# Window-attention backward: turning the gradients of the first quads on TensorE behind the last pair of the step before, instead of inside the softmax

## The chip, the cores and the metric

The kernel runs on one core of a Trainium2 chip. The metric is the device time of one execution in microseconds. Before the change the median of four runs is 1995.97 us (1989.96, 1994.89, 1997.04 and 1997.92). Engines are named as in the profile: PE is TensorE, DVE VectorE, ACT ScalarE, POOL GpSimd, SP SyncE (here a queue that only issues DMAs). PEld is PE's loading of weights, which runs beside the matmuls.

## The reference

The input is an image of 256 x 256 positions with 384 channels, cut into 1024 windows of 8 x 8 = 64 positions. Each window is one attention with a single head. Wanted are the output and the gradients with respect to `x`, `wqkv` and `wo`, all in bfloat16.

```
xw  = windows of x                        # (1024, 64, 384)
q, k, v = split(xw @ wqkv)
p   = softmax(q k^T * 384**-0.5)
out = (p v) @ wo
out_1, out_2, out_3 = gradients of out by x, wqkv, wo, for the given grad_out
```

## The kernel before

The weights are multiplied with each other once, at the start (`A = wq wk^T * scale`, `AT` its transpose, `B = wv wo`, `BT` its transpose), so that a window needs only the tokens `x` and the incoming gradient `d`. Eight windows form a quad: four tiles `t` of 128 tokens, each with two windows. There are 128 quads, `sts[0]` to `sts[127]`. Per quad, `xq` and `dq` are the tokens and the gradients as loaded; `xT` and `dT` are the same turned, with the channels on the partitions.

`step(c, b, a, ahead)` (line 330) works on three quads at once. The main loop calls it for i = -1 to 128 with c = quad i-1, b = quad i, a = quad i+1 and ahead = quad i+3. All engines run in the order in which the code is written (`manual_schedule`, line 417). In one step:

- For b: `scores` (line 179) multiplies `yz` with `xT` into the PSUM tile `sd`; `soft` 0 to 5 (line 191) are the softmax and its backward part on DVE and ACT, ending in the tile `ps`; between them `uv` (line 230) makes two products per tile, `uq` and `vq`, each brought out of PSUM by ACT (line 238). `turn` (line 240) turns `ps` into `PS` by a DMA.
- For a: `project(0)` (line 160), called z here, multiplies `BT` with all of `dT`, ACT brings it out (line 170). `project(1)`, called y, multiplies `A` with `xT` (brought out at line 172). Both go to the tile `yz`, which `scores` of the next step needs whole, and which `to_tokens` turns by a DMA into `tok`.
- For c: `attend` (line 250) makes the outputs `o` and `d` and the operands of the weight gradients, for tiles (0, 1) between z and y and for tiles (2, 3) at the end of the step. ACT brings out `o` and `d` (line 273), POOL issues their stores.
- From step 4 on, `filler` (line 322) runs the products of the weight gradients (`gf_group`, groups of three quads) twice in each step, on PE and DVE. Steps 0 to 3 have none.

The turned gradients `dT` come from a DMA on SP (`load_turn`, line 129) for quads 4 to 127. For quads 0 to 3 (`G_ON_PE` = 4) PE makes them: `turn_on_pe` (line 137) issues, for each tile, three PE transposes into a PSUM tile `pt` (line 141) and one copy out (lines 91 and 89: DVE for t = 0 and 2, ACT for t = 1 and 3). Quad 0 is turned before the loop. Quads 1 to 3 are turned by `A(grad_turn)` in steps 0 to 2, between the products of tile 2 and tile 3 in `uv`. `woT_sb`, the turned `wo` that only the end of the kernel uses, is made in step 0 behind z: nine transposes (line 97), two copies on DVE and one on ACT.

All PSUM tiles come from `ring`, eight slots of one bank. A slot is given out in the order in which the code frees the slots; a product into a slot waits until the copy out of the slot's last content has ended. `dT` has two slots, `xT` three, `xq` ten.

Of the kernel before, what the change touches and what calls it, by code (L numbers as in the profile page):

```python
# [22 lines left out]
def kernel(  # L23
# [38 lines left out]
    wo_sb = grp.tile([P, CK, C], BF16, tag="Wq", name="wo_sb")  # L62
    wT = [grp.tile([P, CK, C], BF16, tag="Uq", name="wT") for part in range(3)]
    woT_sb = const.tile([P, CK, C], BF16)
# [9 lines left out]
    def fetch_weights():  # L74
        nc.sync.dma_start(out=w_sb[:, :, columns(2)], in_=w_in[:, :, columns(2)])
        nc.scalar.dma_start(out=wo_sb[:], in_=wo.rearrange("(m p) n -> p m n", p=P))
        for k in (0, 1):
            nc.scalar.dma_start(out=w_sb[:, :, columns(k)], in_=w_in[:, :, columns(k)])

    def warm_up(n):  # L80
        zero = B_sb[:].rearrange("p m c -> p (m c)")[:, 0:4 * P]
        nc.vector.memset(zero, 0.0)
        for i in range(n):
            pt = ring.tile([P, 4 * P], F32, tag="r", name="warm")
            nc.tensor.matmul(pt[:], lhsT=zero[:, 0:P], rhs=zero, start=True, stop=True)

    def copy_out(i, out, in_):
        if i % 2:
            nc.scalar.copy(out=out, in_=in_)
        else:  # L90
            nc.vector.tensor_copy(out=out, in_=in_)  # L91

    def turn_blocks(dst, src, first=0):
        for k in range(CK):
            pt = ring.tile([P, C], BF16, tag="r", name="pt")
            for m in range(CK):
                nc.tensor.transpose(pt[:, m * P:(m + 1) * P], src[:, m, (first + k) * P:(first + k + 1) * P], ident[:])
            copy_out(k, dst[:, k, :], pt[:])

    def weight_product(dst, left, right, sc):  # L100
        for mr in range(CK):
            pc = ring.tile([P, C], F32, tag="r", name="pc")
            for mc in range(CK):
                nc.tensor.matmul(pc[:], lhsT=left[:, mc, mr * P:(mr + 1) * P], rhs=right[:, mc, :],
                                 start=(mc == 0), stop=(mc == CK - 1))
            if sc is not None:
                nc.scalar.activation(out=dst[:, mr, :], in_=pc[:], func=ACT.Copy, scale=sc)
            else:
                copy_out(mr, dst[:, mr, :], pc[:])

    def weight_rest():
        weight_product(B_sb, wT[2], wo_sb, None)
        weight_product(AT_sb, wT[1], wT[0], scale)
# [8 lines left out]
    def load(st):  # L122
        st["xq"] = xq = grp.tile([P, QUAD, C], BF16, tag="xq", name="xq", bufs=2 * GQ + 4)
        st["dq"] = dq = qp.tile([P, QUAD, C], BF16, tag="dq", name="dq", bufs=6)
        for t in range(QUAD):
            nc.sync.dma_start(out=xq[:, t, :], in_=windows(x, st, 2 * t))
            nc.gpsimd.dma_start(out=dq[:, t, :], in_=windows(grad_out, st, 2 * t))  # L127

    def load_turn(st):
        st["xT"] = qp.tile([P, QUAD, CK, P], BF16, tag="xT", name="xT", bufs=3)  # L130
        st["dT"] = qp.tile([P, QUAD, CK, P], BF16, tag="dT", name="dT")
        for src, dst, on_pe in (("dq", "dT", G_ON_PE), ("xq", "xT", X_ON_PE)):
            if st["i"] >= on_pe:
                nc.sync.dma_start_transpose(out=st[dst][:].rearrange("p t m k -> p (t m) k"),
                                            in_=st[src][:].rearrange("p t c -> p (t c)"))

    def turn_on_pe(st, src, dst):
        for t in range(QUAD):
            pt = ring.tile([P, CK, P], BF16, tag="r", name="pt")
            for m in range(CK):  # L140
                nc.tensor.transpose(pt[:, m, :], st[src][:, t, m * P:(m + 1) * P], ident[:])
            copy_out(t, st[dst][:, t, :, :], pt[:])

    def grad_turn(st):
        if 0 < st["i"] < G_ON_PE:
            turn_on_pe(st, "dq", "dT")

    ALL = False
    split = [ALL]
# [38 lines left out]
    def over_k(ap, n=P):  # L188
        return ap.unsqueeze(2).broadcast_to([n, QUAD, WT])

    def soft(st, step):
        sd = st["sd"]
        if step == 0:
# [113 lines left out]
    def gf_group(sts, last=False):  # L307
        n = len(sts) * QUAD
        for f in range(2):
            if last:  # L310
                final[f] = grp.tile([P, CK, C], BF16, tag="Uq", name="GFb")
            for ma in range(CK):
                pw = ring.tile([P, C], F32, tag="r", name="pg")
                for i in range(n):
                    st, t = sts[i // QUAD], i % QUAD
                    product(pw[:], st["xq"][:, t, ma * P:(ma + 1) * P], st["UW"[f] + "q"][:, t, :], i == 0, i == n - 1)
                nc.vector.tensor_tensor(out=GF_acc[:, f, ma, :], in0=pw[:], in1=GF_acc[:, f, ma, :], op=ALU.add)  # L317
                if last:
                    nc.vector.tensor_copy(out=final[f][:, ma, :], in_=GF_acc[:, f, ma, :])
                yield  # L320

    def filler(n):
        while n and fill:
            try:
                next(fill[0])
                n -= 1
            except StopIteration:
                fill.pop(0)

    def step(c, b, a, ahead):  # L330


        def on(st):
            return (lambda f, *r: f(st, *r)) if st is not None else (lambda f, *r: None)
        C_, B, A = on(c), on(b), on(a)
        B(scores)
        B(soft, 0)
        if b is not None and c is None:
            weight_rest()
        B(uv, 0, 0)  # L340
        B(uv, 0, 1)
        B(soft, 1)
        B(uv, 1, 0)
        B(uv, 1, 1)
        B(soft, 2)
        B(soft, 3)
        B(uv, 2, 0)
        B(uv, 2, 1)
        A(grad_turn)
        B(uv, 3, 0)  # L350
        B(uv, 3, 1)
        B(soft, 4)
        for mo in range(CK):
            A(project, 0, mo)
        if b is not None and c is None:
            turn_blocks(woT_sb, wo_sb)
        B(soft, 5)
        B(turn)
        if ahead is not None:
            load(ahead)  # L360
        filler(1)
        C_(attend, (0, 1))
        split[0] = True
        for mo in range(CK):
            A(project, 1, mo)
        A(to_tokens)
        filler(1)
        split[0] = ALL
        C_(attend, (2, 3))

    G_ON_PE, X_ON_PE = 4, 1
    EV = {"z": "AAA", "y": "AAA", "u": "AAAA", "v": "AAAA", "o": "AAAA", "U": "DDDD", "W": "DDDD", "d": "AAAA"}
    quads = [(row, col) for row in range(0, H, 2 * WIN * QUAD) for col in range(0, W, WIN)]
    sts = [{"at": q, "i": i} for i, q in enumerate(quads)]
# [42 lines left out]
    with tc.manual_schedule(engines=MANUAL):  # L417
        fetch_weights()
        warm_up(9)
        load(sts[0])  # L420
        make_identity(nc, ident[:])
        load(sts[1])
        load(sts[2])
        load_turn(sts[0])
        load_turn(sts[1])
        turn_blocks(wT[2], w_sb, 2 * CK)
        weight_product(BT_sb, wo_sb, wT[2], None)
        turn_on_pe(sts[0], "dq", "dT")
        turn_on_pe(sts[0], "xq", "xT")
        turn_blocks(wT[0], w_sb, 0)  # L430
        turn_blocks(wT[1], w_sb, CK)
        weight_product(A_sb, wT[0], wT[1], scale)
        nc.vector.memset(GF_acc[:], 0.0)
        held = []
        last = None
        get = lambda i: sts[i] if 0 <= i < n else None
        for i in range(-1, n + 1):
            if 0 <= i < n - 2:
                load_turn(sts[i + 2])
            step(get(i - 1), get(i), get(i + 1), get(i + AHEAD) if i >= 0 else None)  # L440
            if i > 0:
                held.append(sts[i - 1])
                sts[i - 1] = None
            if held and i == n:
                last = gf_group(held, True)
            elif len(held) == GQ:
                fill.append(gf_group(held))
                held = []
        split[0] = False
        filler(1 << 30)  # L450
        weight_gradients(last)
# [30 lines left out]
```

## Time and profile before

| | |
|---|---|
| median of four runs | 1995.97 us |
| the profiled execution | 1997.92 us, of which the span of the trace is 1996.1 us |
| PE busy | 1970.3 us, 99% of the span |
| ACT busy | 1462.8 us, 73% |
| DVE busy | 1260.3 us, 63% |
| granted TensorE clock | 0.998 in the mean |

The start of the matmuls of `scores` (tile `sd`) marks the steps: 18.32 us for step 0, then 33.99, 48.97, 63.25, 76.14, 91.26 and 106.39 for steps 1 to 6. From step 4 on a step takes 15.13 us in most cases. The profile lists busy time of each engine, a timeline of its instructions (start, duration, engine, line, operation; in square brackets the idle time before it and what ended it), and the waits summed by engine and releaser. A row with "x3" holds three instructions that follow each other, and its duration is that of all three.

### The profile page before, as it was taken

The page shows a single profiled execution, that of the slowest core. Times are in us where ns is not written, and L with a number is a line of the kernel's source. Part 1 is how long each engine was busy: PE and PEld are TensorE (multiplying, and loading weights), DVE is VectorE, ACT ScalarE, POOL GpSimd, SP SyncE. Part 2 cuts the span into 40 slices and gives each one's busy share as a digit, 9 for nine tenths or more (in the row PEclk, how much of TensorE's full clock was granted, in tenths as well). Part 3 has the DMA queues.
Part 4 walks back from the last instruction along what each step waited for, and adds up shares of the span by engine and source line. Part 5 has one row for each costly group of instructions (what it writes and reads, how often), then busy time and mean ns, then how long its engine had stood idle before and what let it go on. Part 6 is the DMA issues. An engine that isn't in the chain of part 4 may idle for free.

```text
span 1996.1 us, 52529 instructions
## 1 busy us (share of the span) xinstructions
PE 1970.3 (99%) x19487; PEld 1126.2 (56%) x19487; DVE 1260.3 (63%) x2860; ACT 1462.8 (73%) x3357; POOL 1124.6 (56%) x2054
## 2 busy tenths in 40 slices
PE   8999999999999999999999999999999999999999
PEld 4555555555555555555555555555555555555555
DVE  4666665666656666666665666666666665666666
ACT  6877776777777777777776777777777776777774
POOL 3655555555555555555655565556555655555553
PEclk9999999999999999999999999999999999999999
DMA  7999999999999999999999999999999999999994
GB/s 170 217 202 223 211 221 207 214 208 223 216 219 220 221 207 224 219 216 215 219 220 211 216 208 225 216 220 220 223 211 222 215 220 201 213 230 217 214 210 107
DMA packets 1036032, 423.66 MB, mean 212 GB/s; under 512 B 918016, under 2 KB 1011200, under 8 KB 1035776
## 3 DMA queue, kind: packets, MB, share of 16 engines
q1 hardware_dynamic: 935984, 267.85, 81.2%
q0 software_dynamic: 98304, 151.39, 30.9%
q8 instruction: 152, 2.49, 0.6%
q10 hardware_dynamic: 1488, 1.08, 0.2%
q14 instruction: 104, 0.85, 0.2%
HBM read 101.84 MB, written 101.84 MB: 102 GB/s over the span
## 4 chain that ended last, share of the span: by engine, by line
PE 89%; DMA 8%; issue 2%; POOL 1%; ACT 0%; DVE 0%; SPq 0%; ACTq 0%; POOLq 0%
PE pj L156 33%; PE pg L156 12%; PE pj L154 12%; PE pg L154 11%; PE pd L267 6%; PE pu L262 5%; DMA dT<-dq 5%; PE sd L156 4%; PE pw L262 4%; DMA PS<-ps 1%; DMA out_dram<-o 1%; POOL dq L127 0%; DMA dq<-in_grad_out_dram 0%; PE pd L262 0%; PE pe L384 0%
## 5 line engine op out<-in xcount | busy, mean ns | idle before, releaser
L301 POOL DMA_DIRECT2D out_dram<-o x256 | 139.5, 545 | 668.3 <-ACT o L273 665.4
L317 DVE TENSOR_TENSOR GF_acc<-pg,GF_acc 128x384 f32<-128x384 f32 x258 | 144.0, 558 | 527.9 <-PE pg L154 373.9
L273 ACT CAST o<-po 128x384 bf16<-128x384 f32 x512 | 221.7, 486 | 248.0 <-issue 245.7
L156 PEld LDWEIGHTS <-xT 128*128 128x128 bf16 x3072 | 291.7, 98 | 183.2 <-issue 1.5
L156 PE MATMUL pj<-AT_sb,xT 128*128 128x384 bf16 x1536 | 333.3, 326 | 0.8 <-DVE dT L91 0.8
L156 PE MATMUL pj<-B_sb,xT 128*128 128x384 bf16 x1536 | 333.4, 326 | 0.0
L127 POOL DMA_DIRECT2D dq<-in_grad_out_dram x512 | 273.0, 539 | 83.9 <-DMA out_dram<-o 35.3
L156 PE MATMUL pj<-dT,BT_sb 128*128 128x512 bf16 x1152 | 270.9, 380 | 12.7 <-DMA dT<-dq 7.6
L154 PE MATMUL pj<-xT,A_sb 128*64 128x512 bf16 x2304 | 271.9, 381 | 0.0
L238 ACT CAST uq<-pj 128x384 bf16<-128x384 f32 x512 | 247.6, 484 | 30.0 <-PE pj L156 25.9
L238 ACT CAST vq<-pj 128x384 bf16<-128x384 f32 x512 | 249.9, 488 | 2.2
L273 ACT CAST d<-pd 128x384 bf16<-128x384 f32 x512 | 226.9, 509 | 0.2 <-ACT o L273 0.2
L156 PEld LDWEIGHTS <-xq 128*128 128x128 bf16 x1572 | 153.9, 98 | 115.3 <-issue 1.4
L154 PEld LDWEIGHTS <-xq 128*64 128x64 bf16 x3000 | 167.8, 110 | 89.1 <-issue 0.2
L216 ACT COPY ps<-Pb 64x256 bf16<-64x256 bf16 x256 | 103.3, 403 | 149.7 <-DVE Pb L213 148.2
L172 ACT CAST yz<-pj 128x512 bf16<-128x512 f32 x384 | 208.0, 653 | 2.0 <-PE pj L154 1.6
L170 ACT CAST yz<-pj 128x512 bf16<-128x512 f32 x384 | 206.7, 638 | 3.0 <-PE pj L156 1.5
L156 PEld LDWEIGHTS <-BT_sb 128*128 128x128 bf16 x1152 | 111.5, 98 | 140.0 <-DMA dT<-dq 14.2
L154 PEld LDWEIGHTS <-A_sb 128*64 128x64 bf16 x2304 | 132.1, 110 | 98.2 <-issue 2.2
L156 PE MATMUL pg<-Uq,xq 128*128 128x384 bf16 x1032 | 182.1, 327 | 0.0
L262 PE MATMUL pu<-xq,PS 64*64 64x384 bf16 x1024 | 174.9, 335 | 3.8 <-DMA PS<-ps 3.5
L267 PE MATMUL pd<-tok,ps 128*64 128x384 bf16 x1024 | 177.7, 344 | 0.0
(87 smaller groups left out, 3391.0 us busy)
## 6 DMA issues: line engine op xcount, KB each, us to landing
xq<-in_x_dram SPq DMA_DIRECT2D x512, 96.0 KB, 4.1
dq<-in_grad_out_dram POOLq DMA_DIRECT2D x512, 96.0 KB, 4.0
out_dram<-o POOLq DMA_DIRECT2D x256, 96.0 KB, 4.3
out_dram<-o POOLq DMA_DIRECT2D x512, 48.0 KB, 4.4
out_dram<-d POOLq DMA_DIRECT2D x256, 96.0 KB, 4.5
out_dram<-d POOLq DMA_DIRECT2D x512, 48.0 KB, 4.5
tok<-yz SPq DMA_TRANSPOSE x128, 8.3
PS<-ps SPq DMA_TRANSPOSE x128, 4.8
```

Source lines behind the costliest of these rows:

```text
L127: nc.gpsimd.dma_start(out=dq[:, t, :], in_=windows(grad_out, st, 2 * t))
L154: nc.tensor.matmul(out[h], lhsT=lhsT[:, h], rhs=rhs, start=start, stop=stop)
L156: nc.tensor.matmul(out, lhsT=lhsT, rhs=rhs, start=start, stop=stop)
L170: ENG[EV["z"][mo]](out=yz[:, mo, :, 0:4:3, :], in_=pj[:])
L172: ENG[EV["y"][mo]](out=yz[:, mo, :, 1:3, :], in_=pj[:])
L216: nc.scalar.copy(out=ps[h, :, w, :], in_=Pb[h, :, :])
L238: cp(out=dst[:, t, :], in_=pj[:])
L262: nc.tensor.matmul(at[o, :], lhsT=turned(st, lhs, t, h), rhs=st[rhs][h, t, :], **{"start": True, "stop": True, **fl})
L267: nc.tensor.matmul(pd[outer if w == 0 else 1 - outer][o, :], lhsT=st["ps"][:, t, w, :], rhs=st["tok"][:, :, t, w, :], **flags)
L273: nc.scalar.copy(out=sb[:], in_=src[outer][:])
L301: nc.gpsimd.dma_start(out=windows(dst, st, 2 * t0 + 1), in_=sb[:])
L317: nc.vector.tensor_tensor(out=GF_acc[:, f, ma, :], in0=pw[:], in1=GF_acc[:, f, ma, :], op=ALU.add)
```

## The change

`grad_turn` goes away. The main loop calls `turn_on_pe` itself, right after `step`, for quad i+2 where that is quad 1, 2 or 3. Quad 1 is therefore turned at the end of step -1, quad 2 at the end of step 0 and quad 3 at the end of step 1, each behind the last thing that the step does on PE and ahead of the next step's `scores`. `turn_blocks(woT_sb, wo_sb)` moves from step 0 to the end of step 1, behind the turn of quad 3. The number of instructions on each engine is the same; SP's and POOL's queues hold the same instructions in the same order.

```diff
-    def grad_turn(st):
-        if 0 < st["i"] < G_ON_PE:
-            turn_on_pe(st, "dq", "dT")
...
         B(uv, 2, 0)
         B(uv, 2, 1)
-        A(grad_turn)
         B(uv, 3, 0)
         B(uv, 3, 1)
         B(soft, 4)
         for mo in range(CK):
             A(project, 0, mo)
-        if b is not None and c is None:
-            turn_blocks(woT_sb, wo_sb)
         B(soft, 5)
         B(turn)
...
             step(get(i - 1), get(i), get(i + 1), get(i + AHEAD) if i >= 0 else None)
+            if 0 < i + 2 < G_ON_PE:
+                turn_on_pe(sts[i + 2], "dq", "dT")
+            if i == 1:
+                turn_blocks(woT_sb, wo_sb)
             if i > 0:
```

## The prediction

> **What bounds the kernel now.** I read the page's busy times first, then PE's waits in the stretch that the change touches, then the timeline of steps 0 to 3, and last SP's queue. Busy times and PE's waits from 14 to 80 us (us in total, times, longest):
>
> ```profile
> PE 1970.3 (99%) x19487; PEld 1126.2 (56%) x19487; DVE 1260.3 (63%) x2860; ACT 1462.8 (73%) x3357; POOL 1124.6 (56%) x2054
> ...
> PE pj L156 <- ACT dT L89: 4.7, 3, 1.6
> PE sd L156 <- ACT yz L172: 0.9, 2, 0.4
> PE pj L156 <- DVE dT L91: 0.8, 3, 0.3
> ```
>
> PE is the bound over the whole; its idle time is 1996.1 - 1970.3 = 25.8 us, and 4.7 + 0.8 = 5.5 us of it stand at the three turns: z waits for ACT's copy of `dT`, and the last `uv` product for a slot held by a turn. That is what the diff suggests can be won. The timeline of step 0 and of step 3, which is a step with neither a turn nor a filler, says how much of it really can:
>
> ```profile
> 18.32 0.30 PE L156 MATMUL sd<-xT,yz 128*128 128x64 bf16 x2
> 19.07 0.82 PE L156 MATMUL sd<-xT,yz 128*128 128x64 bf16 x22 [0.45 <-ACT yz L172]
> 25.57 0.83 PE L141 MATMUL pt<-ident,dq 128*128 128x128 bf16 x12
> 27.71 0.48 ACT L238 CAST uq<-pj 128x384 bf16<-128x384 f32 x1
> 28.46 0.88 ACT L89 COPY dT<-pt 128x384 bf16<-128x384 bf16 x2
> 29.39 2.10 PE L156 MATMUL pj<-dT,BT_sb 128*128 128x512 bf16 x9 [1.58 <-ACT dT L89]
> 32.01 0.48 ACT L89 COPY woT_sb<-pt 128x384 bf16<-128x384 bf16 x1
> 32.81 1.88 ACT L172 CAST yz<-pj 128x512 bf16<-128x512 f32 x3 [0.31 <-PE pj L154]
> 34.74 0.81 PE L156 MATMUL sd<-xT,yz 128*128 128x64 bf16 x22 [0.45 <-ACT yz L172]
> 48.97 0.87 PE L156 MATMUL sd<-xT,yz 128*128 128x64 bf16 x24
> 63.25 0.87 PE L156 MATMUL sd<-xT,yz 128*128 128x64 bf16 x24
> 69.03 0.48 ACT L238 CAST uq<-pj 128x384 bf16<-128x384 f32 x1
> 70.52 1.61 ACT L170 CAST yz<-pj 128x512 bf16<-128x512 f32 x3
> 73.80 1.71 ACT L172 CAST yz<-pj 128x512 bf16<-128x512 f32 x3
> 76.36 0.88 ACT L273 CAST d<-pd 128x384 bf16<-128x384 f32 x2
> 76.14 0.87 PE L156 MATMUL sd<-xT,yz 128*128 128x64 bf16 x24
> ```
>
> Step 2, with a turn, takes 63.25 - 48.97 = 14.28; step 3 takes 76.14 - 63.25 = 12.89. The turn costs PE 12 transposes (0.67: the next `uv` starts at 38.99 after a turn begun at 38.32) and waits of 0.27 and 1.58, together 2.52. Yet the step without it is only 1.39 shorter. The other 1.13 goes to ACT: in step 3 the products of `attend` follow ACT's casts through the ring (its first half takes from 69.89 to the start of y at 72.65, 2.76, against 58.45 to 59.70, 1.25, in step 2). In the first steps, without fillers, ACT is next in line behind the stall.
>
> **The change part by part.** PE's clock is 1.00 in all these stretches, so durations carry over.
>
> *Turn of quad 1, to the end of step -1.* PE ends y near 18.32 and then waits for ACT's last `yz` cast until 19.07; only two of `scores`' 24 matmuls run before. The 12 transposes (0.67) end at 18.99. Their cost is 0 to 0.1; if ACT's cast were not the cover, 0.67. Quad 1's gradients are issued by POOL from 4.11 on, and land in 4.0 in the median. ACT's two copies (0.88) fall in its idle 1.88 from 19.01 to 20.89, DVE's two in its idle 4.57 up to 19.92.
>
> *Step 0, turn and `woT` gone from inside.* ACT's chain to the first `uq` cast after the exponent (27.71) does not change: the cast waits for `ps`, which waits for `Pb` on DVE, ahead of the turn's copies. From there ACT runs on: in step 3 the first z cast starts 70.52 - 69.03 = 1.49 behind that cast, so here at 29.20. Six `yz` casts follow; three take 1.61 to 1.88, so they end between 29.20 + 3.3 and 29.20 + 3.76, at 32.5 to 33.0. Check by what left ACT: 0.88 for `dT`, 0.48 for `woT`, and the waits 0.13 and 0.31, together 1.80. `scores` of step 1 resumes 0.05 behind the last cast: 32.55 to 33.0 instead of 34.74. I take 32.85: 1.9 gained (1.7 to 2.2). The late thing is now ACT, not the stall: PE would be through y at about 30.65.
>
> *Turn of quad 2, to the end of step 0.* 0.67 on PE from 30.65 to 31.3, inside PE's wait for ACT: 0. Cover gone: 0.67. ACT's two copies stand ahead of the first `uq` cast, which comes 1.34 behind `scores` (36.08 - 34.74): 0.88 fits.
>
> *Step 1, turn gone; turn of quad 3 and `woT` at its end.* The inside becomes step 3's 12.89. At the end come 12 + 9 transposes, 21 x 0.056 = 1.17, ahead of `scores`. They and `sd` take all eight slots that `attend` just used, so one waits for ACT's last `d` cast (77.24 in step 3's clock, 1.1 behind the end of `attend`): the whole takes 1.17 to 1.45. Sum 14.06 to 14.34, against 48.97 - 34.68 = 14.29 before. I take 14.25: nothing gained (-0.05 to 0.23). ACT's three copies (1.36) end at 78.6 in that clock, `uq` needs it at 79.0.
>
> *Step 2, turn gone.* 14.28 becomes 12.89: 1.39.
>
> Sum: 1.9 + 0 + 1.4 = 3.3 us (2.9 to 3.8) by the start of step 3, not 5.5. From step 3 on both kernels have the same instructions and the same reuse of ring slots. The queues: SP's `PS` of quad 0 goes at about 29.5 instead of 33.70, and its later entries follow `ps` and `yz`, so SP moves with PE; POOL's stores follow `o` and `d`. The profiled execution's 1997.92 becomes 1994.6; it lies 1.95 above the median, and on the median I predict 1995.97 - 3.3 = 1992.7.
>
> [...]
>
> **The rivals.** *Whole stall.* All 5.5 us goes and the two hidden turns give another 2 x 0.67: 6.9, time 1989.1. For it speaks the wait table; against it the 12.89 of step 3, and ACT's unbroken casts from 69.03 to 77.24. It needs the `attend` of steps 1 and 2 to run at 1.25 instead of 2.76.
>
> *Taken back by SP.* SP's queue stands nearly full, and this is how it falls behind `scores`:
>
> ```profile
> 62.85 6.46 SPq L176 DMA_TRANSPOSE tok<-yz  x1
> ...
> 78.82 5.74 SPq L176 DMA_TRANSPOSE tok<-yz  x1
> ...
> 314.20 4.32 SPq L176 DMA_TRANSPOSE tok<-yz  x1
> ```
>
> `tok` is issued 0.4 before `scores` at 63.25, 2.68 behind it in step 4 (76.14), 8.57 in step 8 (137.68, 146.25). Steps 7 to 9 take 16.16, 15.80 and 15.33: 1.9 over 15.13, where PE waits for `dT` and `PS`. If the earlier PE only meets an SP that is no earlier, the 3.3 returns as waits there: 1996.0. Against it: SP is at its data's heels in steps 2 and 3. With the change `tok` of step 2 can go at about 45.0 instead of 48.37, and the round of 14.48 behind it ends at 59.5 instead of 62.85, a shift of 3.35, as PE's.
>
> *Slower.* The same queue, over its limit. At 314.20 `tok` goes 8.87 behind `scores` (305.33), and in that step PE waits 1.98 for `PS`; the step takes 18.86, 3.7 over. Another at 1053.79 takes 18.98. Quiet steps have lags of 5 to 8. If the earlier start puts SP's transposes beside the loads and stores so that the lag crosses about 8.6 more often, each crossing costs up to 3.7. Three more decide: -3.3 + 3 x 3.7 = +7.8, 2003.8. Nothing in the profile makes three more likely than three fewer.
>
> **How the numbers follow.** 0.3% is 6.0 us, about what a measurement of this kernel can tell from no change; the four runs spread over 8.0, and all steps after 4 lose 17.9 over 15.13 in the profiled one, much of it in a few long ones. Chances: forecast 0.58 (1992.7), whole stall 0.17 (1989.1), taken back 0.14 (1996.0), slower 0.11 (2003.8). The likeliest alone lies within 1992.2 to 1993.1 by its own bounds, and with half the spread of the runs to each side within 1988.7 to 1996.7. The range takes in most of the whole stall and the case taken back, with some spread: 1987.5 to 1999.5. Faster by over 0.3%, below 1990.0: nearly two thirds of the whole stall and a quarter of the forecast, 0.11 + 0.15 = 0.26. Slower, above 2002.0: 0.09. Between: 0.65.
>
> **What would show it.** Right: no wait of z for `dT` in steps 0 to 2; `scores` at about 32.8, 47.0, 59.9 and 72.8 for steps 1 to 4; a wait of 1.2 to 1.7 for ACT's `yz` ahead of `scores` of step 1; `attend`'s first half near 2.7 in steps 1 and 2; 15.13 in quiet steps. Wrong: steps 1 and 2 below 12.5 (whole stall); step 4 on time, but steps 6 to 9 longer by 3 together (taken back); more steps above 16 (slower); a granted clock below 1.00 from 14 to 49.

## The result and the profile after

The changed kernel takes 1991.39 us (median of 53 runs), the kernel before 1994.8 us (79 runs): 3.4 us less. The means differ by 4.1 us; their ratio is 0.9979, with a 95% interval of 0.9970 to 0.9989, so between 2.2 and 6.0 us. The prediction was 3.3 us less, 1992.7 us from a median of 1995.97.

The busy times and PE's waits from 14 to 80 us of the changed kernel (us in total, times, longest; its lines behind `turn_on_pe` have numbers four smaller than before):

```profile
PE 1969.3 (99%) x19487; PEld 1125.9 (57%) x19487; DVE 1261.0 (63%) x2860; ACT 1461.0 (74%) x3357; POOL 1124.5 (57%) x2054
```

```profile
PE sd L152 <- ACT yz L168: 0.6, 2, 0.3
```

The six waits at the three turns, 5.5 us, are gone. The timeline of the same stretch shows what took their place. The first row, z of quad 0, stands ahead of everything that the change moves and is my zero: in this execution it starts at 13.69, in that of before at 14.21. The difference is not the weights, as an expectation below has it, but a wait of PE for a load of `x` that only the execution of before has:

```profile
11.17 0.34 PE L141 MATMUL pt<-ident,xq 128*128 128x128 bf16 x3 [0.51 <-DMA xq<-in_x_dram]
```

The changed kernel:

```profile
13.69 2.10 PE L152 MATMUL pj<-dT,BT_sb 128*128 128x512 bf16 x9
17.79 0.84 PE L141 MATMUL pt<-ident,dq 128*128 128x128 bf16 x12
18.47 0.89 PE L152 MATMUL sd<-xT,yz 128*128 128x64 bf16 x24
26.01 2.10 PE L152 MATMUL pj<-dT,BT_sb 128*128 128x512 bf16 x9
27.18 0.48 ACT L234 CAST uq<-pj 128x384 bf16<-128x384 f32 x1
28.67 1.61 ACT L166 CAST yz<-pj 128x512 bf16<-128x512 f32 x3
30.10 1.65 ACT L168 CAST yz<-pj 128x512 bf16<-128x512 f32 x3
30.11 0.84 PE L141 MATMUL pt<-ident,dq 128*128 128x128 bf16 x12
31.80 0.81 PE L152 MATMUL sd<-xT,yz 128*128 128x64 bf16 x22 [0.29 <-ACT yz L168]
44.63 0.84 PE L141 MATMUL pt<-ident,dq 128*128 128x128 bf16 x12
45.31 0.76 PE L97 MATMUL pt<-ident,wo_sb 128*128 128x128 bf16 x9
45.91 0.86 PE L152 MATMUL sd<-xT,yz 128*128 128x64 bf16 x24
58.78 0.87 PE L152 MATMUL sd<-xT,yz 128*128 128x64 bf16 x24
71.67 0.87 PE L152 MATMUL sd<-xT,yz 128*128 128x64 bf16 x24
86.80 0.87 PE L152 MATMUL sd<-xT,yz 128*128 128x64 bf16 x24
```

Three things can be read from it. The turn at 17.79 fills a time in which PE waited before. In step 0, PE is through y at about 30.1 and through the turn at 30.8, and `scores` still waits until 31.80: ACT's last cast ends at 30.10 + 1.65 = 31.75. And the turns at 44.63 stand in PE's way: 45.91 - 44.63 = 1.28. From `scores` to `scores`, against before:

| | before | after | gained |
|---|---|---|---|
| first z to `scores` of step 1 (its main part) | 20.53 | 18.11 | 2.42 |
| step 1 | 14.23 | 14.11 | 0.12 |
| step 2 | 14.28 | 12.87 | 1.41 |
| step 3 | 12.89 | 12.89 | 0 |
| first z to `scores` of step 4 | 61.93 | 57.98 | 3.95 |

The profiled spans differ by much more, 1996.1 - 1987.2 = 8.9 us. Of this 3.95 is the change, 0.52 the earlier first z, and the remaining 4.4 the steps from 4 on that take more than 15.13 us: they add up to 17.8 us in the profile before and 13.4 in the one after. Profiles of the same kernel scatter nearly as much: 16.4 in a second one of before, 17.0 in a second one of after. Two single executions could not have shown this change; its share was readable only in the first four steps. The longest step after is step 8 with 19.60, between the two `scores`; its z waited for `dT` and then took 3.69 us instead of 2.10:

```profile
132.19 0.87 PE L152 MATMUL sd<-xT,yz 128*128 128x64 bf16 x24
139.58 3.69 PE L152 MATMUL pj<-dT,BT_sb 128*128 128x512 bf16 x9 [2.61 <-DMA dT<-dq]
151.79 0.87 PE L152 MATMUL sd<-xT,yz 128*128 128x64 bf16 x24
```

### The profile page after: what moved, and what is told of

It reads as the page before. It is cut to its first block, busy times and chain, and to the rows that moved or that the text cites. A ratio compares the mean times of both kernels' runs of the same rounds, so it can differ in the third digit from the quotient of the medians.

```text
span 1987.2 us, 52531 instructions
## 1 busy us (share of the span) xinstructions
PE 1969.3 (99%) x19487; PEld 1125.9 (57%) x19487; DVE 1261.0 (63%) x2860; ACT 1461.0 (74%) x3357; POOL 1124.5 (57%) x2054
## 4 chain that ended last, share of the span: by engine, by line
PE 91%; DMA 6%; ACT 2%; DVE 1%; issue 0%; SPq 0%; ACTq 0%
PE pj L152 33%; PE pj L150 12%; PE pg L152 12%; PE pg L150 12%; PE pd L263 6%; PE pu L258 5%; PE sd L152 5%; PE pw L258 4%; DMA dT<-dq 4%; DMA PS<-ps 2%; ACT uq L234 1%; ACT vq L234 0%; DMA xq<-in_x_dram 0%; PE pd L258 0%; ACT yz L166 0%
```

## The experiments

All times of steps below are read like those of the table, from the first z of quad 0.

**The parts alone.** The turns moved, `woT` left where it was:

```diff
-            if i == 1:
-                turn_blocks(woT_sb, wo_sb)
...
+        if b is not None and c is None:
+            turn_blocks(woT_sb, wo_sb)
         B(soft, 5)
```

> The turns are moved as in the changed kernel, woT stays in step 0. Times are counted from the first z of quad 0 (14.21 us before, 13.69 after), so that the arrival of the weights does not enter; scores of step 4 stand at 61.9 before and at 58.0 after. ACT theory: woT puts 0.48 of ACT's work and 0.5 of PE's back into step 0, so scores of step 1 go 0.4 to 0.6 later than in the changed kernel (18.5 to 18.7 against 18.1), and the end of step 1 gets 0.5 to 0.8 shorter; step 4 stays within 0.3 of 58.0. Rival (the move of woT brings a part of the gain): step 4 stands 0.5 or more behind 58.0.

`scores` of step 1 came at 32.38 - 13.87 = 18.51, 0.4 later than in the changed kernel; step 1 was 0.6 shorter; step 4 stood at 71.64 - 13.87 = 57.77, against 57.98 in the changed kernel. Moving `woT` brings nothing: what it frees in step 0, and 0.2 more, it costs at the end of step 1.

`woT` moved alone, the turns left in the softmax (the diff is the other half of the change):

> Only woT is moved to the end of step 1, the turns stay in the softmax. Counted from the first z of quad 0. ACT theory: step 0 gets 0.4 to 0.7 shorter, step 1 longer by the same, the three waits of z for the turn (1.58 each) stay, and scores of step 4 stand within 0.3 of 61.9. Rival (woT was a part of the gain): step 4 at 61.4 or less.

Step 4 stood at 78.81 - 13.61 = 65.20, 3.3 later than the ACT theory had it, and further still from the rival. This is its z of steps 0 and 1, and the windows around them (us, then busy time of PE, PEld, DVE, ACT and POOL with the number of instructions, the granted TensorE clock, the share of the DMA engines, GB/s):

```profile
28.78 3.51 PE L156 MATMUL pj<-dT,BT_sb 128*128 128x512 bf16 x9 [1.59 <-ACT dT L89]
42.67 3.73 PE L156 MATMUL pj<-dT,BT_sb 128*128 128x512 bf16 x9 [1.58 <-ACT dT L89]
```

```profile
22.00:26.00 4.00, 4.00 (x35) 2.67 (x33) 1.03 (x4) 3.06 (x7) 0.00 (x0) 1.00 0.91 180
26.00:30.00 4.00, 2.15 (x10) 0.82 (x9) 3.20 (x9) 3.43 (x9) 0.00 (x0) 0.91 0.00 0
30.00:34.00 4.00, 4.00 (x22) 1.44 (x22) 0.00 (x0) 2.13 (x5) 0.00 (x0) 0.66 0.45 107
42.00:46.00 4.00, 3.33 (x9) 1.10 (x8) 1.17 (x3) 2.55 (x6) 0.00 (x0) 0.62 0.43 83
```

Behind the same stall of 1.58 us as before, the granted clock was 0.62 and 0.66 in the mean of two of these windows, and the two z took 3.51 and 3.73 us instead of 2.10; y of step 0 took 2.36 instead of 2.13. The third z, in step 2, was not slow. Take off 1.41 + 0.23 + 1.63 = 3.27, and step 4 stands at 61.93, where the ACT theory had it. That leaves the question whether the stall did this or chance.

**The stall and the clock.** ACT's copies of the turn made twice, so that z waits longer, and the kernel before once more:

```diff
             copy_out(t, st[dst][:, t, :, :], pt[:])
+            if t % 2 and st["i"]:
+                copy_out(t, st[dst][:, t, :, :], pt[:])
```

> The kernel before, with ACT's two copies of dT made twice at each of the three turns: 0.9 us more of ACT's work, and z waits about 2.4 instead of 1.58. If a stall of that length takes the clock down, as it did at two of three turns in the run that moved woT alone (z took 3.51 and 3.73 us instead of 2.10, granted clock 0.62 to 0.66), then at least two of the three z here take 3.4 or more, and steps 1 and 2 are 2 or more longer than 14.98 and 14.28. If those two were a chance of the run and not of the stall, all z take 2.1, and the steps are 0.9 longer.

> The kernel before once more, to see how often its own stall of 1.58 us takes the clock down. If the phase of the clock's control against the kernel is what decides, one or two of the three z behind the stalls take 3.4 us or more, and scores of step 4 stand 1.4 to 3.5 behind the 61.9 of the first profile; if the stall is too short on its own, all three take 2.1 and step 4 stands at 61.9.

The three z of the longer stall:

```profile
29.61 2.76 PE L158 MATMUL pj<-dT,BT_sb 128*128 128x512 bf16 x9 [2.60 <-ACT dT L89]
45.00 3.56 PE L158 MATMUL pj<-dT,BT_sb 128*128 128x512 bf16 x9 [2.60 <-ACT dT L89]
61.76 3.71 PE L158 MATMUL pj<-dT,BT_sb 128*128 128x512 bf16 x9 [2.60 <-ACT dT L89]
```

All three were hit: they took longer than 2.10, two of them about as long as the two z above. Steps 1 and 2 (first matmul to first matmul) took 17.45 and 16.92 against 14.98 and 14.28. The granted clock was 0.996 in the mean of this execution, against 0.997 to 0.999 in the eight of the kernel before beside it. So behind the longer stall in this place, 2.60 us, z was slow three times of three, though all in one execution. The length of the wait does not decide alone. The z of step 8 above was slow behind a wait of 2.61 us, with a granted clock of 0.58 in the mean from 140 to 144 us; a z shown below, behind the same eight `uv` products, waited 2.62 and took 2.12. The kernel before, once more, kept 2.10 at all three, with step 4 at 61.94. In all, of nine stalls of 1.58 us two were hit, both in the same execution. Why those two stays open; the phase that an expectation above names is not shown by any run. That some executions of the kernel before lose 1.4 to 1.6 us at such a z, and that the change spares them, is likely but not shown: none of the six stalls in its two profiles was hit, and the interval of the ratio holds 3.95 us with and without it.

**Is ACT what limits the first steps?** z of quads 1 to 4 brought out by DVE:

```diff
-            ENG[EV["z"][mo]](out=yz[:, mo, :, 0:4:3, :], in_=pj[:])
+            ENG["D" if 0 < st["i"] <= 4 else EV["z"][mo]](out=yz[:, mo, :, 0:4:3, :], in_=pj[:])
```

> The changed kernel, with the casts of z of quads 1 to 4 on DVE instead of ACT (steps 0 to 3). It takes 1.6 us of casts off ACT in each of these steps. ACT theory (ACT sets the length of the steps without fillers): steps 1, 2 and 3 get 0.8 to 1.3 shorter than 14.1, 12.87 and 12.89, scores of step 1 come 0.5 to 0.9 earlier, and scores of step 4 stand at 53.5 to 55 from the first z, against 58.0. Rival (PE and the softmax set it): these steps change by less than 0.3. For the time: if what is won at the start stays, it is 3 to 4.5 us below the changed kernel, 0.996 of the kernel before; if SP's queue takes it back, SP's tok goes 8 or more behind scores by step 5, steps 4 to 12 are longer by 3 or more together than in the changed kernel, and the time is that of the changed kernel, 0.998.

`scores` of steps 1 to 5, and z of step 4:

```profile
30.54 0.89 PE L152 MATMUL sd<-xT,yz 128*128 128x64 bf16 x24
44.01 0.86 PE L152 MATMUL sd<-xT,yz 128*128 128x64 bf16 x24
56.05 0.87 PE L152 MATMUL sd<-xT,yz 128*128 128x64 bf16 x24
68.10 0.87 PE L152 MATMUL sd<-xT,yz 128*128 128x64 bf16 x24
74.20 2.12 PE L152 MATMUL pj<-dT,BT_sb 128*128 128x512 bf16 x9 [1.32 <-DMA dT<-dq]
84.73 0.87 PE L152 MATMUL sd<-xT,yz 128*128 128x64 bf16 x24
```

Steps 2 and 3 went from 12.87 and 12.89 to 12.04 and 12.05, step 1 (from the main part of `scores`) from 14.11 to 13.47, which is less than expected, and `scores` of step 1 came 1.0 earlier, a little more than expected. Step 4 stood at 68.10 - 13.43 = 54.67. PE's instructions are the same, so ACT's casts set these steps. But the time was 0.9976 of before (0.9954 to 0.9998), no different from the changed kernel's 0.9979: step 4 took 16.63, with PE waiting 1.3 for `dT`. Of the signs named for SP's queue, `tok` stood 7.7 behind `scores` at step 5 (8 was named), but steps 4 to 12 lost 2.5 us over 15.13, less than the 4.5 of the changed kernel's first profile. This run alone did not settle what took the gain back.

**What takes it back?** The changed kernel again, the one just described again, and that one with quads 4 and 5 turned on PE too:

```diff
-    G_ON_PE, X_ON_PE = 4, 1
+    G_ON_PE, X_ON_PE = 6, 1
```

> The changed kernel once more, as the neighbour of the next two and for its clock: no z of steps 0 to 2 above 2.2 us (the stall in the softmax is gone; what idle PE has left at the end of step 0 is 0.6 in two pieces). Scores of step 4 at 57.8 to 58.1 from the first z. Time 0.997 to 0.999 of the kernel before.

> The changed kernel with the casts of z of quads 1 to 4 on DVE, in more rounds beside the changed kernel itself. Its start is 3.3 us shorter up to step 4, but step 4 took 16.63 in its first profile, 1.5 over, with PE waiting 1.3 for dT. If that wait is there again (it follows from SP's queue: dT of quad 5 can't come earlier), 1.5 to 2 us of the 3.3 stay: 1.5 to 2 below the changed kernel, 0.997 of the kernel before. If the wait was chance, step 4 takes 15.13 and 3 us stay.

> The same with quads 4 and 5 also turned on PE, at the ends of steps 2 and 3 (six instead of four quads). It takes two transposes of 1.8 to 2.7 us off SP's queue where that falls behind, and puts 24 transposes (0.67 us per quad) on PE. If SP's queue is what takes back the gain of the start: no wait for dT in step 4, tok less than 7 behind scores in steps 4 and 5, steps 2 and 3 at 12.7 to 12.9, step 4 at 15.13; scores of step 5 then stand at 70.8 to 71.4 from the first z, against 71.3 with four quads. If PE's extra work only adds: scores of step 5 at 72.5 or more, and the time 1 to 1.5 above that kernel.

The changed kernel: step 4 at 71.48 - 13.50 = 57.98, clock 1.00 in all windows from 14 to 50 us, ratio 0.9973 (0.9956 to 0.9989). With z on DVE, `scores` of steps 4 and 5 and z between them:

```profile
68.50 0.87 PE L152 MATMUL sd<-xT,yz 128*128 128x64 bf16 x24
75.89 2.12 PE L152 MATMUL pj<-dT,BT_sb 128*128 128x512 bf16 x9 [2.62 <-DMA dT<-dq]
86.42 0.87 PE L152 MATMUL sd<-xT,yz 128*128 128x64 bf16 x24
```

The same with six quads turned on PE:

```profile
69.69 0.86 PE L152 MATMUL sd<-xT,yz 128*128 128x64 bf16 x24
74.29 2.10 PE L152 MATMUL pj<-dT,BT_sb 128*128 128x512 bf16 x9
84.81 0.87 PE L152 MATMUL sd<-xT,yz 128*128 128x64 bf16 x24
```

With z on DVE the wait for `dT` was there again, and longer: step 4 took 17.92. So the 3.3 us that z on DVE wins up to step 4 are met by an SP queue that can't follow; 1.5 and 2.8 us of it were lost in step 4 alone in the two profiles. The ratio of z on DVE was 0.9964 (0.9947 to 0.9981), not to be told from the changed kernel's. With two more turns on PE, steps 2 and 3 take 12.84 and 12.82, but step 4 takes 15.12, `tok` goes 2.1 behind `scores` of step 5 instead of 7.6, and steps 4 to 9 lose nothing. `dT` of step 4 no longer comes by SP, so its wait had to go; that no other took its place in this profile shows SP keeping pace. Up to step 5 the two turns cost about what they save. `scores` of step 5 stands at 71.35, against 72.61 with four quads in the run beside it but 71.30 in the first run with four. The ratio is 0.9941 (0.9918 to 0.9964), the median 1986.91 us. This version beats both kernels; against the changed kernel beside it the mean is 4.9 us lower (1986.07 of 6 runs, 1990.98 of 12, with standard errors of 0.9 each). Against z on DVE with four quads it is 4.0 lower (1990.09 of 12 runs, standard error 1.3), more than the profiles show: by step 10 it is 0.1 and 1.6 ahead of the two. Where the rest comes from was not found.

**Can SP's queue be relieved for good?** Three tries on the changed kernel, for the long steps of the steady state. The loads of x from SP to POOL:

```diff
-            nc.sync.dma_start(out=xq[:, t, :], in_=windows(x, st, 2 * t))
+            (nc.gpsimd if st["i"] > 4 else nc.sync).dma_start(out=xq[:, t, :], in_=windows(x, st, 2 * t))
```

> The changed kernel, with the loads of x from quad 5 on issued by POOL instead of SP, which takes 2.5 to 3 us of 15 off SP's round. If the long steps (13 to 18 us in all over 15.13 per execution) come from SP's queue being full: tok goes less than 3 behind scores from step 6 on, the long steps shrink to under 5 us in all, and the time is 0.991 to 0.994 of the kernel before. If the DMA engines are what is full: SP's transposes get longer by what the loads leave, tok stays 5 to 9 behind, the long steps stay, and the time is 0.997 to 0.999. If POOL's queue, where the loads now stand behind stores, brings x late: PE waits for xT, and the time is above 1.000.

The loads of grad_out from POOL to SP, and from POOL to ACT:

```diff
-            nc.gpsimd.dma_start(out=dq[:, t, :], in_=windows(grad_out, st, 2 * t))
+            (nc.sync if st["i"] > 4 else nc.gpsimd).dma_start(out=dq[:, t, :], in_=windows(grad_out, st, 2 * t))
```

> The changed kernel, with the loads of grad_out from quad 5 on issued by SP instead of POOL: the opposite of the run that gave x to POOL and took 15% longer. If what slows SP's transposes is transfers of POOL's queue running beside them, SP's round stays under 15.1 although it issues four loads more (2.5 us), the steps above 15.6 go away, and the time is 0.990 to 0.996 of the kernel before. If SP's issuing itself is what is full: its round grows from about 15 to 17 or more, PE waits for PS and dT in nearly every step, and the time is 1.05 or more.

> The changed kernel, with the loads of grad_out from quad 5 on issued by ACT. As with SP, they leave POOL's queue, but SP's round gets no longer. If POOL's transfers beside the transposes are what slows them: tok goes less than 4 behind scores, and the time is 0.990 to 0.996 of the kernel before. ACT issues four more loads per step (about 2 us, 11.3 busy of 15.13 now): if that makes ACT late, PE waits for ACT's casts, and the time is above 1.00.

All three are far slower: 1.1496 (1.1455 to 1.1536), 1.1601 (1.1574 to 1.1627) and 1.2002 (1.1965 to 1.2040). PE's longest waits in each (x on POOL, then grad_out on SP, then on ACT):

```profile
PE pu L258 <- DMA PS<-ps: 124.5, 73, 4.8
PE pj L152 <- DMA dT<-dq: 90.6, 53, 4.8
```

```profile
PE pj L152 <- DMA dT<-dq: 211.6, 85, 4.7
```

```profile
PE pj L150 <- ACT Uq L279: 272.1, 121, 4.8
```

With x on POOL, SP issues less and is still late. Two issues of `tok` around 510 us there:

```profile
510.43 8.62 SPq L172 DMA_TRANSPOSE tok<-yz  x1
528.04 4.82 SPq L172 DMA_TRANSPOSE tok<-yz  x1
```

One takes 8.62 us against 4.2 to 4.6 in the same stretch of the kernel before, and from issue to landing `tok` takes 13.0 us in the median instead of the changed kernel's 8.4. The second of the three expectations had the direction of that, but not the 15%; waits for `xT`, which the third named, do not show among PE's. With grad_out on SP, its round in this stretch grows to 18.1 (from 508.92 to 526.99), as expected for a queue whose issuing is full. With grad_out on ACT, it is ACT that comes late: from 500 to 800 us it sat idle before its `Uq` cast, 20.4 us ended by `PS`, 17.3 by the loads of grad_out, 20.8 by nothing shown. None of the three relieves a queue without a larger loss elsewhere. In these three the mean granted clock was 0.96 to 0.97 instead of 1.00, so slower work of PE behind the waits is likely a part of the loss; how much was not separated.

## Why the prediction was right

- *The stall goes, and less than its 5.5 us is won.* Right. The reason was ACT: in a step without turn or filler `attend` follows ACT's casts. z on DVE showed it: the same PE work in 0.8 us less in steps 2 and 3, where forecast and measured step agree (12.89; 12.87 and 12.89).
- *Turn of quad 1, cost 0 to 0.1.* Right: `scores` starts 4.78 behind the first z instead of going on at 4.86, and ends at 5.67 as at 5.68.
- *Step 0, 1.9 (1.7 to 2.2).* Mechanism right, size too small: 2.42. The first `uq` cast stands 13.49 behind the first z, as before (13.50), and the z cast 1.49 behind it, as taken from step 3. The term that was off is the six `yz` casts, taken as 3.3 to 3.76 by adding the lengths of two rows of three; they took 31.75 - 28.67 = 3.08, since the second row starts 0.18 before the first ends and none of the casts was stretched (1.61 and 1.65, not up to 1.88). From the end of the turn `scores` was held about 1.0, of which 0.6 show as waits, instead of 1.2 to 1.7 for the same reason.
- *Turn of quad 2, cost 0.* Right, it lies inside that wait.
- *Step 1, 14.25.* It was 14.11; the transposes at its end took 1.28 (1.17 to 1.45 forecast). The forecast set 14.25 against 14.29, counted from 34.68; counted from `scores` at 34.74, step 1 before is 14.23, and 0.12 was gained where nothing was forecast.
- *Step 2, 1.39.* It was 1.41.
- *The sum, 3.3 (2.9 to 3.8).* In the profiles 3.95, just outside the sum's own bounds; 0.5 of the excess is in the casts of step 0, 0.1 in step 1. In the medians it is 3.4. That this lies so near 3.3 is partly luck: an interval of 2.2 to 6.0 can't tell 3.3 from 3.95, and the median before moved by 1.2 between forecast and result.
- *Whole stall.* Wrong for the reason given: the first half of `attend` in step 2 still takes 2.76, from 52.54 to the start of y at 55.30.
- *Taken back by SP.* Not as a whole, for the medians keep 3.4 us. `tok` of step 2 went at 44.0 (45.0 forecast) instead of 48.37, `tok` of step 3 at 58.9 (59.5), and steps 4 to 7 take 15.13. But `tok` of step 4 stood 4.9 and 3.5 behind `scores` in the two profiles of the changed kernel, against 2.7 and 2.8 before, and step 8 of the first was the 19.60 shown above. Steps 4 to 9 lost 4.5 and 1.9 us over 15.13, and 5.5 with the turns alone; in the four profiles that keep the turns in the softmax they lost 1.9 and three times nothing. By step 25 the gain was back: 386.0 and 382.5 from the first z before, 382.1 and 378.9 after, since the kernel before lost more between steps 10 and 25. Whether SP takes back a part for good is open. Of the next 3.3 us, those of z on DVE, step 4 took 1.5 and 2.8. So the case was real.
- *Slower.* Steps above 16 went on coming: 6 and 5 in two profiles of the kernel before, 4 and 9 in two of the changed one. In the times nothing shows that they grew.
- *The clock.* The prediction carried durations over at a clock of 1.00 and named a lower one from 14 to 49 us as a sign against itself. Neither profile of the changed kernel shows a granted clock below 1.00 in a window of 4 us from 14 to 50 us, the end of step 0 included. What the prediction did not weigh is the clock at the stall that the change removes. There, behind a wait of 1.58 us with 12 transposes and two `uv` products in the 2.2 us ahead of it, z was slow twice of nine, both times with `woT` moved alone, and the granted clock was 0.62 to 0.66 in the mean of a window of 4 us around it. What makes the difference between those two and the other seven, no run here separates.

## What to carry to other kernels

A wait that is taken away is worth the time until the next resource ends, not its own length: here 5.5 us of waits went and 3.95 us were won, since ACT's casts ended next. Find a stretch of the same trace that already lacks the wait, and read the worth from it. A gain of a few microseconds in a long kernel has to be read from the stretch that changes, counted from an event that the change doesn't touch, since the rest of one execution scatters by more (13.4 to 17.8 us over 15.13 a step in four profiles of the two kernels). If a second gain in the same place comes to nothing, look which queue had kept pace with the first and can't with the second; here two transposes less on it took away the wait of 1.32 and 2.62 us that had met the second gain.

## What was not expected of the hardware

- Behind a wait of PE of 1.58 us z took 3.51 and 3.73 us instead of 2.10 at two of nine such waits, with a granted clock of 0.66 and 0.62 in the mean of a window of 4 us around them; behind one of 2.60 us it took longer at three of three (2.76, 3.56, 3.71). Elsewhere one of 2.61 was followed by a z of 3.69, with a granted clock of 0.58 in the mean of 4 us, one of 2.62 by a z of 2.12.
- Loads of 48 MB issued from another queue cost 15 to 20% of the whole, in either direction between SP and POOL and from POOL to ACT. With the loads of `x` on POOL the transposes to `tok` took 13.0 us to land instead of 8.4. Which resource they share there was not separated.
- The long steps, 13 to 18 us in all per execution of both kernels, differ from execution to execution. That SP's lag goes with them was seen; what starts one was not found.
